# All steps of an attention and two-layer kernel in a new order, with the small key and query loads split by head

## The chip, the cores and the metric

The kernel runs on one core of one Trainium2 chip. TensorE (PE in the profile) multiplies matrices, VectorE (DVE), ScalarE (ACT) and GpSimd (POOL) work elementwise, and SyncE (SP) issues most of the DMAs. The metric is the time of one execution on the device in microseconds; the median of three runs before the change is 488.42 us (487.62 to 489.02).

## What is computed

All data is float32. First attention with rotary positions over 2 batches, 8 heads, 576 positions and 64 dimensions per head; then a gated product; then a second layer whose middle is a softmax gate and a normalization.

```python
q_rot, k_rot = (rotate(q), rotate(k))      # x1*cos - x2*sin, x1*sin + x2*cos
scores = np.matmul(q_rot, k_rot.transpose(0, 1, 3, 2)) / np.sqrt(D)
attn = np.exp(scores - np.max(scores, axis=-1, keepdims=True))
attn = attn / (np.sum(attn, axis=-1, keepdims=True) + 1e-09)
x = np.matmul(attn, v)                     # reshaped to [1152, 512]
x = (x @ w_a) * (x @ w_b) @ w_out          # 512 -> 1536 -> 512
h = x @ w_in                               # 512 -> 1024
e = np.exp(h - np.max(h, axis=-1, keepdims=True))
solu = h * e / (np.sum(e, axis=-1, keepdims=True) + 1e-09)
ln = (solu - mu) / np.sqrt(var + 1e-06) * g_ln
out = ln @ w_out2                          # 1024 -> 512
```

## The kernel before

**Tiles and stages.** Every matrix product is made of three: each operand is kept as a high part, rounded to TensorE's fast float32 form by a cast, and a low part, the difference between the operand and its high part, and high x high, high x low and low x high are summed. So each operand costs a cast (mostly on ScalarE) and a difference (on VectorE or GpSimd).

Attention goes through eight pairs of heads, u = 0 to 7, with nine blocks of queries each (72 blocks in all). A pair's 576 positions lie as four blocks of 128 for head A, one block "R" with the last 64 positions of both heads, and four blocks for head B. For a pair, SyncE loads keys, queries and values (`lk`, `lq`, `lv`); the rotation is three passes (`rk0` to `rk2` for keys, `rq0` to `rq2` for queries, lines 320, 325 and 327) on GpSimd or VectorE; the rotated queries are written twice side by side by a DMA (`qd`, line 334); keys are cast and differenced (`kh` line 345, `kl` line 356) and both are transposed by TensorE (`kA`, `qA`, `R`, `kB`, `qB`, lines 373 and 379). Per query block: the scores (`qk`, line 446), the row maximum on VectorE (`mx`, line 455), the exponential on ScalarE (`ex`, line 463), transposes (`tp`, line 476), the high part on ScalarE (`ph`, line 490), the low part on VectorE (`pl`, line 494), and then the product with the values (`pv`, line 525). A quotient and a split write the pair's result into the input x of the next layer (`xa`, `xb`, `xc`).

The first layer begins with three groups of weights multiplied plainly (`AB`, line 716, three column ranges each, 24 instructions a range). Each product has two halves in one of two PSUM buffers; ScalarE copies one half out (`ab`, line 820) and VectorE multiplies it with the other (`g`, line 823), which frees the buffer. The other nine groups use Strassen's scheme (`P1` to `P7`, line 943), for which sums and differences of the input are made once (`s1`, `s3`, `sb`, `s2a` and so on, line 747), cast (`sh`, line 860) and differenced (`sl`). Then comes the product with `w_out` (`X`, line 1013, in three column ranges of 12 steps). The second layer multiplies tile 0 of nine row tiles plainly (`H`, line 1038) and the other eight in pairs by Strassen's scheme (`Q1` to `Q7`, line 1131). Its weight differences are summed on VectorE (`u1` to `u4`, line 747, buffer `tfh`), cast (`uh`), negated (`un`, line 1067), and completed by a DMA that adds `tfh` to the negated high part (`ua`, line 1070, issued from GpSimd). There are four such adding DMAs; the two of one k share a `tfh`, and the next k's `tfh` takes the same memory. Each tile then goes through maximum, exponential, product, statistics and normalization (`hx`, `he`, `hm`, `hs`, `hn`, lines 1159 to 1185), transposes (`L`, line 1193), and the last product (`O`, line 1229).

**What sets the order.** Nothing is scheduled at run time or by the compiler. The string SCHEDULE names every step, `name.index` with a last `.1` where a step goes to GpSimd instead of VectorE, and the program is written in exactly that order; each engine takes its own instructions from it in turn, and SyncE its DMAs. Steps wait for each other by semaphores, so a step whose input is late holds up everything behind it on its engine. The string was put out by a planner that is not part of the kernel.

The start is written out before the schedule: the first loads go out from SyncE and ScalarE (lines 613 to 619), TensorE turns over an identity matrix as warm-up, and `rka` rotates blocks 0 to 4 of the first keys, `kha` casts them and `kla` makes their low part.

Of the kernel before, what the change touches and what calls it, by code (L numbers as in the profile page):

```python
# [20 lines left out]
B, H, S, D = 2, 8, 576, 64  # L21
# [6 lines left out]
REM = 512  # L28
# [7 lines left out]
wm1.0 cs.0 lv.0 wm2.0 rka0.0 ll.0 rka1.0 rka2.0 rqx0.0 kha.0 rqx1.0 rqx2.0 kla.0 kA_0.0 kA_1.0 rqa0.0 rqa1.0  # L36
rqa2.0 qdx.0 qda.0 qAx0.0 qA_0.0 R_0.0 qAh0.0 rkb0.0 rkb1.0 rkb2.0 khb.0 klb.0 rqb0.0 R_1.0 rqb1.0 wm3.0 qAl0.0
R_2.0 rqb2.0 qAh1.0 qk.0 qAl1.0 qdb.0 wm4.0 qk.1 mx.0 ex.0 rq0.1.1 mx.1 rk0.1 ex.1 qk.2 kB_0.0 kB_1.0 mx.2 ex.2
rq1.1 rq2.1.1 rk1.1 rk2.1.1 qk.3 mx.3 qB_0.0 qB_1.0 qB_2.0 tp.0 tp.1 qk.4 ph.0 ex.3 lv.1 ph.1 pl.0 mx.4 t4A_0.0
t4A_1.0 tp.2 qk.5 qd.1 ph.2 qA_0.1 kh.1 pl.1 tp.3 ex.4 qk.6 mx.5 qA_1.1 vh.0 t4A_2.0 kl.1.1 ex.5 pl.2 ld.0  # L40
qA_2.1 lk.2 rk0.2.1 mx.6 ph.3 pl.3 t4R_0.0 kB_0.1 kB_1.1 tp.4 ex.6 qk.7 mx.7 lq.2 t4R_1.0 t4R_2.0 tp.5 vl.0
kA_0.1 R_0.1 ph.4 pl.4 qk.8 ph.5 mx.8 kA_1.1 rk1.2.1 lk.3 pv00_0.0 ex.7 tp.6 rk2.2.1 pv00_1.0 R_1.1 qk.9 rq0.2.1
rq1.2.1 rq2.2.1 R_2.1 pl.5 pv01_0.0 qd.2 pv01_1.0 ph.6 pl.6 ex.8 mx.9 sa.0 pv00_2.0 qk.10 kh.2 rs_0.0 qB_0.1
lq.3 pv00_3.0 lv.2 ex.9 tp.7 kl.2.1 mx.10 pv01_2.0 pv01_3.0 qk.11 mx.11 rs_1.0 t4B_0.0 qB_1.1 qB_2.1 ex.10 qk.12
rs_2.0 ph.7 ex.11 pl.7 vh.1 tp.8 mx.12 t4B_1.0 t4B_2.0 ph.8 kA_0.2 rk0.3.1 ex.12 rq0.3.1 pl.8 vl.1.1 rq1.3.1
qk.13 tp.9 kA_1.2 ph.9 qA_0.2 mx.13 pl.9 rk1.3.1 rk2.3.1 qk.14 pv10_0.0 tp.10 tp.11 qA_1.2 lk.4 ex.13 ph.10
pv10_1.0 qA_2.2 pv11_0.0 mx.14 ph.11 pl.10 pv10_2.0 ex.14 pv11_1.0 pv11_2.0 pl.11 pv10_3.0 tp.12 t4R_0.1
# [36 lines left out]
pv00_1.6 mx.62 ex.61 vl.7.1 ex.62 p3.0 R_2.7 p4.0 tp.60 pv01_0.6 pv01_1.6 ph.60 qB_0.7 qk.63 sa.6 rs_0.6 qk.64
# [1237 lines left out]
```

## Time and profile before

| | |
|---|---|
| median of three runs | 488.42 us |
| profiled execution | 487.74 us |
| its span, first to last instruction | 485.8 us |
| TensorE busy | 469.9 us, 97% of the span |
| VectorE busy | 407.2 us, 84% |
| ScalarE busy | 349.7 us, 72% |
| GpSimd busy | 199.0 us, 41% |
| mean granted TensorE clock | 1.000 |
| moved by DMA | 48.04 MB, 99 GB/s on average |

The shares are averages over stages with different limits. Attention ends near 162 us, the plain products run from there to about 197 us, Strassen's products to 302, the product with `w_out` to 379, and the second layer to the end. TensorE's busy time counts an instruction until its modelled end, so a busy TensorE in attention is not TensorE at its peak: an instruction of 288 columns takes 183 ns on average there (58.7 us for 320 of them in the scores) and 147 ns in Strassen's products (31.6 us for 216).

### The profile page before, as it was taken

Reading aid. Unit: us, or ns where it says so; the run is one execution under the profiler, and the core shown is the slowest. Engines: PE = TensorE matmul, PEld = TensorE weight load, DVE = VectorE, ACT = ScalarE, POOL = GpSimd, SP = SyncE. Lnnn points to the kernel's source line nnn. Section 1 sums busy time; section 2 is a strip of 40 time slices with the busy share of each in tenths; the row PEclk is TensorE's granted clock in tenths of the full one; section 3 lists DMA queues with packets and bytes.
Section 4 is the critical chain, followed back from the end, with each engine's and each line's share of the span. In section 5 each row is a group of like instructions: output and inputs, shape, how many; then the busy total and the mean of one; then the engine's idle time right before and its main releaser. Section 6 shows DMA issues by size and latency. Waiting matters only on the chain.

```text
span 485.8 us, 8453 instructions
## 1 busy us (share of the span) xinstructions
PE 469.9 (97%) x3109; PEld 441.9 (91%) x3109; DVE 407.2 (84%) x617; ACT 349.7 (72%) x655; POOL 199.0 (41%) x171
## 2 busy tenths in 40 slices
PE   8899899999989989999999999999999989999996
PEld 7789899999989979999999999999999778888886
DVE  5999899999999769988786898776786999978671
ACT  4899899999989275767878888787896763535321
POOL 1798989779433240022225113222211475431100
PEclk9999999999999999999999999999999999999999
DMA  5624414222203403414235654245337520100011
GB/s 141 185 65 108 116 32 129 75 50 73 57 7 106 148 26 120 142 52 123 89 132 169 217 175 173 89 173 188 127 120 175 92 81 1 44 23 22 23 43 43
DMA packets 47506, 48.04 MB, mean 99 GB/s; under 512 B 23979, under 2 KB 40938, under 8 KB 46954
## 3 DMA queue, kind: packets, MB, share of 16 engines
q1 hardware_dynamic: 45946, 44.53, 29.5%
q0 software_dynamic: 576, 2.10, 2.4%
q10 hardware_dynamic: 944, 0.89, 0.6%
q8 instruction: 24, 0.39, 0.3%
q14 instruction: 16, 0.13, 0.1%
HBM read 39.01 MB, written 4.49 MB: 90 GB/s over the span
## 4 chain that ended last, share of the span: by engine, by line
PE 69%; DVE 9%; ACT 8%; POOL 6%; DMA 4%; issue 3%; ACTq 0%; SPq 0%; DVEq 0%; POOLq 0%
PE x L1013 11%; PE out L1229 10%; PE pb L943 9%; PE pc L943 6%; PE pa L943 6%; PE s L446 5%; PE pv L525 5%; PE h L1131 5%; PE ab L716 4%; PE t L476 3%; PE lt L1193 2%; PE hc L1131 2%; ACT e L463 2%; DMA hT<-tfh 2%; DVE pT L494 1%
## 5 line engine op out<-in xcount | busy, mean ns | idle before, releaser
L1013 PE MATMUL x<-gs,wx 128*128 128x384 f32 x432 | 75.2, 334 | 0.0
L1013 PEld LDWEIGHTS x<-gs,wx 128*128 128x128 f32 x432 | 74.9, 188 | 0.1
L446 PE MATMUL s<-kS,qS 128*128 128x288 f32 x320 | 58.7, 309 | 2.2 <-ACT e L463 2.1
L455 DVE TENSOR_REDUCE nm<-s 128x1 f32<-128x576 f32 x72 | 53.9, 750 | 2.0 <-PE s L446 0.9
L463 ACT ACTIVATE e<-s,nm 128x576 f32<-128x576 f32 x72 | 53.5, 744 | 2.5 <-DVE nm L455 2.2
L169 ACT ACTIVATE f<-f 128x1024 f32<-128x1024 f32 x48 | 50.9, 1062 | 0.9
L1229 PE MATMUL out<-wout,lnT 128*128 128x512 f32 (+1 forms) x240 | 51.5, 371 | 0.0
L446 PEld LDWEIGHTS s<-kS,qS 128*128 128x128 f32 x320 | 45.2, 189 | 4.3 <-ACT e L463 3.5
L494 DVE TENSOR_TENSOR pT<-t,pT 128x512 fp32r<-128x512 f32 x72 | 48.3, 682 | 0.8 <-ACT pT L490 0.2
L1229 PEld LDWEIGHTS out<-wout,lnT 128*128 128x128 f32 x240 | 41.4, 189 | 7.2
L525 PE MATMUL pv<-pT,V 128*128 128x288 f32 x288 | 46.5, 302 | 0.6 <-DVE pT L494 0.2
L490 ACT CAST pT<-t 128x512 fp32r<-128x512 f32 x72 | 40.7, 582 | 2.8 <-PE t L476 2.3
L476 PE MATMUL t<-ident,e 128*128 128x128 f32 x288 | 41.9, 274 | 0.2
L525 PEld LDWEIGHTS pv<-pT,V 128*128 128x128 f32 x288 | 39.9, 188 | 1.5 <-DVE pT L494 0.4
L716 PE MATMUL ab<-xT,wab 128*128 128x384 f32 x216 | 38.8, 336 | 1.7 <-DVE g L823 1.2
L716 PEld LDWEIGHTS ab<-xT,wab 128*128 128x128 f32 x216 | 37.3, 188 | 2.6 <-DVE g L823 1.8
L476 PEld LDWEIGHTS t<-ident,e 128*128 128x128 f32 x288 | 33.5, 141 | 2.5 <-DVE pT L494 1.1
L177 DVE SCALAR_TENSOR_TENSOR f<-raw,f 128x1024 int32<-128x1024 int32 x26 | 34.1, 1310 | 0.4
L179 DVE SCALAR_TENSOR_TENSOR f<-raw,f 128x1024 int32<-128x1024 int32 x26 | 32.5, 1248 | 0.4
L943 PE MATMUL pb<-sums_x,wT 128*128 128x288 f32 x216 | 31.8, 296 | 0.0
L943 PE MATMUL pa<-xT,wB 128*128 128x288 f32 x216 | 31.6, 295 | 0.0
L167 ACT ACTIVATE f<-raw 128x1024 f32<-128x1024 f32 x24 | 27.7, 1153 | 4.7 <-DMA raw<-in_moe_w_b_dram 2.2
(215 smaller groups left out, 1027.7 us busy)
## 6 DMA issues: line engine op xcount, KB each, us to landing
raw<-in_moe_w_out_dram SPq DMA_DIRECT2D x10, 1024.0 KB, 4.8
raw<-in_moe_w_a_dram SPq DMA_DIRECT2D x12, 512.0 KB, 3.6
raw<-in_moe_w_b_dram SPq DMA_DIRECT2D x24, 256.0 KB, 4.2
raw<-in_moe_w_in_dram SPq DMA_DIRECT2D x4, 1024.0 KB
kraw<-in_k_dram SPq DMA_DIRECT2D x16, 128.0 KB, 2.2
qd<-in_q_dram SPq DMA_DIRECT2D x16, 128.0 KB, 3.1
vraw<-in_v_dram SPq DMA_DIRECT2D x8, 256.0 KB
wd<-f SPq DMA_DIRECT2D x4, 512.0 KB
```

The costliest lines, as they stand in the source:

```text
L169: act.activation(_raw(t), _raw(t), AF.Copy, scale=2.0 ** -SHIFT)
L446: nc.tensor.matmul(s[:, c, :KC], qS[u % 2][:, a, off:off + P], kS[u % 2][:, h, c * KC:(c + 1) * KC], start=(m == 0), stop=(m == last),)
L455: nc.vector.tensor_reduce(t, ps[n][:, :, :KC], axis=AX.XY, op=ALU.max, negate=True)
L463: nc.scalar.activation(t.rearrange("p (c n) -> p c n", c=2), ps.pop(n)[:, :, :KC], AF.Exp, bias=nm.pop(n), accum_out=sums[u][:, i:i + 1],)
L476: nc.tensor.transpose(t[:, j, :], e[n][:, j * P:(j + 1) * P], ident)
L490: nc.scalar.copy(hi, src)
L494: nc.vector.tensor_tensor(lo, src, _raw(hi), op=ALU.subtract)
L525: nc.tensor.matmul(o[:, :KC], w[:, h, 4 if m == 8 else m % 4].rearrange("p a d -> p (a d)"), t[:, m, c * KC:(c + 1) * KC], start=(m == 0), ...
L716: nc.tensor.matmul(pab[f, t][:, m, :CW], wf[:, a, (kk, 4 + (kk + 2) % 4)[m], :], xT[kk][:, xa, t * CW:(t + 1) * CW], start=(kk == a == xa ...
L943: nc.tensor.matmul(dst[:, c, :KC], w[:, a, k * P:(k + 1) * P], x(k, xa)[:, c * KC:(c + 1) * KC], start=(fresh and k == a == xa == 0), stop ...
L1013: nc.tensor.matmul(px[t, m][:, :CW], w[:, a], r[:, ga], start=(f == 0 and a == ga), stop=(f == NF - 1 and a == 1),)
L1229: nc.tensor.matmul(po[i, part][:, cols], lnT[i][:, la, kk, :], w[:, a, cols], start=(kk == la == a == 0), stop=(kk == NK2 - 1 and la == 1),)
```

## The change

Three edits. The whole SCHEDULE string is replaced by another, which holds the same steps with three new ones (`rkr0` to `rkr2`) and some of them on the other of VectorE and GpSimd. The planner that put it out now takes the adding DMAs as a single file, one after the other; the planner is not in the kernel, so this shows in the string alone. The last rows of keys and queries of every pair are loaded by two DMAs of 64 rows, as those of pair 0 were before, instead of one of 128. And the rotation of the first keys' blocks 0 to 4 is taken apart into blocks 0 to 3 (`rka`) and block 4 (`rkr`).

```diff
@@ -287,9 +287,7 @@
-        if "R" in parts and u > 0:
-            eng.dma_start(out=t[:, 4, :], in_=src[b, h0:h0 + 2, REM:S, :])
-        elif "R" in parts:
+        if "R" in parts:
             for j in range(2):
                 eng.dma_start(out=t[64 * j:64 * j + 64, 4, :], in_=src[b, h0 + j, REM:S, :])
@@ -654,7 +652,8 @@
-        add(f"rka{j}.0", rope, nc.vector, 0, k0, "k", 0, 5, (j,))
+        add(f"rka{j}.0", rope, nc.vector, 0, k0, "k", 0, 4, (j,))
+        add(f"rkr{j}.0", rope, nc.vector, 0, k0, "k", 4, 5, (j,))
@@ -33,112 +33,112 @@
-wm1.0 cs.0 lv.0 wm2.0 rka0.0 ll.0 rka1.0 rka2.0 rqx0.0 kha.0 rqx1.0 rqx2.0 kla.0 kA_0.0 kA_1.0 rqa0.0 rqa1.0
...
+rka0.0 ll.0 rka1.0 cs.0 rka2.0 rkr0.0 rkr1.0 rkr2.0 rqx0.0 kha.0 rqx1.0 rqx2.0 wm1.0 wm2.0 rqa0.0 rqa1.0 kla.0
...
```

Of the steps that change their engine, these matter in attention: the first and last pass of pair 1's rotation (`rq0.1`, `rk2.1`) go from GpSimd to VectorE, the low part of pair 0's values (`vl.0`) from VectorE to GpSimd. Among the input's sums for Strassen's scheme four go from GpSimd to VectorE and one the other way.

At three places the order reads as follows. The first is ScalarE where the plain products begin, from the cast of the second group's weights (`wab`); `a` is the copy of a product's half, `sums_x` the cast of an input sum, `f` a step of unpacking weights. Before:

```order
L192 CAST wab_2650<-f 128x1024
L820 ACTIVATE a_0_2677<-ab_0_2504 128x384
L860 CAST sums_x<-sums_f_2642 128x576
L820 ACTIVATE a_1_2681<-ab_1_2652 128x384
L860 CAST sums_x<-sums_f_2640 128x576
L167 ACTIVATE f<-raw 128x1024
L169 ACTIVATE f<-f 128x1024
L820 ACTIVATE a_2_2748<-ab_2_2698 128x384
```

and in the changed kernel:

```order
L192 CAST wab_2667<-f 128x1024
L819 ACTIVATE a_0_2669<-ab_0_2494 128x384
L819 ACTIVATE a_1_2697<-ab_1_2671 128x384
L819 ACTIVATE a_2_2726<-ab_2_2700 128x384
L167 ACTIVATE f<-raw 128x1024
L169 ACTIVATE f<-f 128x1024 x2
L819 ACTIVATE a_0_2795<-ab_0_2735 128x384
L167 ACTIVATE f<-raw 128x1024
L859 CAST sums_x<-sums_f_2657 128x576
```

The two casts that stood between the three copies stand behind a fourth copy now.

The second is GpSimd from the cast of pair 1's values (`V`) to the rotation of pair 3; `t2k` and `t2q` are the first passes for keys and queries, `kraw` and `qd` the loaded keys and queries. Before:

```order
L347 CAST V_577<-vraw_326 128x10x64
L320 TENSOR_TENSOR t2k_3_594<-kraw_450,s_sb 128x576
L320 TENSOR_TENSOR t2q_3_598<-qd_518,s_sb 128x576
L365 TENSOR_TENSOR V_577<-vraw_326,V_577 128x10x64
L325 TENSOR_TENSOR qd_518<-qd_518,c_sb 128x9x64
L325 TENSOR_TENSOR kraw_450<-kraw_450,c_sb 128x576
```

and in the changed kernel:

```order
L345 CAST V_568<-vraw_440 128x10x64
L318 TENSOR_TENSOR t2k_3_577<-kraw_486,s_sb 128x576
L323 TENSOR_TENSOR kraw_486<-kraw_486,c_sb 128x576
L363 TENSOR_TENSOR V_568<-vraw_440,V_568 128x10x64
L318 TENSOR_TENSOR t2q_3_672<-qd_544,s_sb 128x576
L323 TENSOR_TENSOR qd_544<-qd_544,c_sb 128x9x64
```

The first pass over pair 3's queries has moved behind a pass over the keys and behind the values' low part.

The third is GpSimd around the four adding DMAs (`hT<-tfh`); `gs` is a low part for the product with `w_out`, the first number in its name the step it belongs to. Before:

```order
L747 TENSOR_TENSOR gs_5_4555<-g_2639,gs_5_4555 128x384
L747 TENSOR_TENSOR gs_6_4571<-g_3462,gs_6_4571 128x384
L1070 DMA hT_4577<-tfh_4529 128x1024
L1070 DMA hT_4537<-tfh_4529 128x1024
L1070 DMA hT_4732<-tfh_4714 128x1024
L1070 DMA hT_4739<-tfh_4714 128x1024
```

and in the changed kernel:

```order
L746 TENSOR_TENSOR gs_3_4537<-g_2654,gs_3_4537 128x384
L1069 DMA hT_4592<-tfh_4512 128x1024
L1069 DMA hT_4636<-tfh_4512 128x1024
L746 TENSOR_TENSOR gs_9_4666<-g_3744,gs_9_4666 128x384
L1069 DMA hT_4715<-tfh_4706 128x1024
L1069 DMA hT_4748<-tfh_4706 128x1024
```

The first two stand behind the low part of step 3 instead of step 6, and a low part of step 9 stands between the pairs. In the schedule the first comes four steps of the product before the second (`X.2.4` to `X.2.7`), where before it was two (`X.2.9` and `X.2.10`, with the first half of tile 0's product).

## Rows read from the trace of the kernel before

**Rows 1.** Windows: start:end, length, busy time (instructions) of each engine, clock, DMA
```profile
60.00:132.00 72.00, 71.22 (x574) 68.08 (x573) 69.60 (x121) 69.58 (x177) 57.06 (x45) 1.00 0.28 72
...
168.00:180.00 12.00, 10.32 (x57) 9.36 (x56) 7.12 (x10) 6.83 (x9) 6.47 (x4) 1.00 0.25 84
...
197.00:356.00 159.00, 159.00 (x1092) 158.51 (x1091) 130.62 (x159) 125.98 (x166) 40.38 (x30) 1.00 0.42 144
...
397.00:482.00 85.00, 84.91 (x427) 70.88 (x425) 64.03 (x108) 32.88 (x64) 22.06 (x29) 1.00 0.09 27
```
**Rows 2.** Chain of waits (first row) and timeline, the start: start, us, what
```profile
1.76 3.46 DMA kraw<-in_k_dram
...
5.35 0.49 DVE L320 TENSOR_TENSOR t2k<-kraw,s_sb 128x320 f32<-128x320 f32 x1 [3.78 <-DMA kraw<-in_k_dram]
...
6.16 0.40 ACT L341 COPY s_sb<-s_sb 128x256 f32<-128x256 f32 x1
...
6.93 0.46 ACT L345 CAST kd<-kraw 128x320 fp32r<-128x320 f32 x1 [0.37 <-DVE kraw L327]
```
**Rows 3.** Groups by line and form, VectorE, 0 to 180: busy us, mean ns, idle
```profile
L747 DVE TENSOR_TENSOR sums_f<-xT 128x1152 f32<-128x1152 f32 x2 | 2.7, 1354 | 0.1
...
L823 DVE TENSOR_TENSOR g<-ab,a 128x384 f32<-128x384 f32 x3 | 1.7, 552 | 4.7 <-ACT a L820 4.7
...
L195 DVE TENSOR_TENSOR wab<-f,wab 128x1024 fp32r<-128x1024 f32 x1 | 1.2, 1212 | 0.0
L365 DVE TENSOR_TENSOR V<-vraw,V 128x640 fp32r<-128x640 f32 x1 | 0.9, 930 | 0.0
...
L320 DVE TENSOR_TENSOR t2k<-kraw,s_sb 128x576 f32<-128x576 f32 x1 | 0.7, 749 | 0.0
...
L320 DVE TENSOR_TENSOR t2k<-kraw,s_sb 128x256 f32<-128x256 f32 x1 | 0.4, 425 | 0.0
...
L320 DVE TENSOR_TENSOR t2q<-qd,s_sb 128x64 f32<-128x64 f32 x1 | 0.2, 225 | 0.0
```
**Rows 4.** Timeline, GpSimd and TensorE, 38 to 53 us
```profile
38.59 1.44 POOL L320 TENSOR_TENSOR t2q<-qd,s_sb 128x576 f32<-128x576 f32 x1 [2.88 <-DMA qd<-in_q_dram]
...
52.64 0.54 PE L373 MATMUL qtkA<-ident_r,kd 128*128 128x128 f32 x4 [1.26 <-POOL kd L356]
```
**Rows 5.** Line 325 on GpSimd: ns min/median/max, first and last start
```profile
L325 POOL TENSOR_TENSOR kraw<-kraw,c_sb x6: 1409/1424/1432, 24.5 to 103.7; 128x576 f32<-128x576 f32 x6
```
**Rows 6.** Timeline, 166 to 180 us
```profile
166.66 3.75 POOL L747 TENSOR_TENSOR sums_f<-xT 128x1152 f32<-128x1152 f32 x1 [12.26 <-DMA raw<-in_moe_w_b_dram]
...
171.94 0.68 ACT L860 CAST sums_x<-sums_f 128x576 fp32r<-128x576 f32 x1 [4.66 <-POOL sums_f L747]
...
173.04 0.56 DVE L823 TENSOR_TENSOR g<-ab,a 128x384 f32<-128x384 f32 x1 [4.68 <-ACT a L820]
...
174.78 4.09 PE L716 MATMUL ab<-xT,wab 128*128 128x384 f32 x22 [0.51 <-DVE wab L195]
...
179.86 16.92 PE L716 MATMUL ab<-xT,wab 128*128 128x384 f32 x96 [0.99 <-DVE g L823]
```
**Rows 7.** Adding DMAs' landings (first row), then timeline, 376 to 394 and 470 us
```profile
DMA to landing us min/median/max: 4.6/4.9/7.6
...
376.13 1.29 DVE L747 TENSOR_TENSOR tfh<-f 128x512 f32<-128x512 f32 x2 [2.53 <-DMA hT<-tfh]
...
381.82 1.21 PE L1038 MATMUL h<-wh,x2T 128*128 128x512 f32 x4 [0.35 <-DVE wh L195]
...
390.68 2.92 DVE L1185 TENSOR_SCALAR et<-et,mv,rs 128x1024 f32<-128x1024 f32 x1 [0.21 <-POOL rs L1180]
...
393.65 1.09 PE L1193 MATMUL lt<-ident,et 128*128 128x128 f32 x8 [1.59 <-DVE et L1185]
...
470.38 0.81 DVE L1185 TENSOR_SCALAR et<-et,mv,rs 128x1024 f32<-128x1024 f32 x1 [0.73 <-POOL rs L1180]
```
**Rows 8.** Line 291's DMA issues on SyncE's queue: ns min/median/max, first and last
```profile
L291 SPq DMA_DIRECT2D kraw<-in_k_dram x7: 554/566/587, 10.5 to 93.0; - x7
```

More of the change, by code (lines that the diff above doesn't have):

```diff
@@ L141 @@
[L141 removed]
+rka0.0 ll.0 rka1.0 cs.0 rka2.0 rkr0.0 rkr1.0 rkr2.0 rqx0.0 kha.0 rqx1.0 rqx2.0 wm1.0 wm2.0 rqa0.0 rqa1.0 kla.0
+rqa2.0 qdx.0 kA_0.0 qAx0.0 qda.0 R_0.0 kA_1.0 rkb0.0 rkb1.0 rkb2.0 qA_0.0 rqb0.0 wm3.0 qAh0.0 qAl0.0 rqb1.0
+rqb2.0 lv.0 qdb.0 R_1.0 R_2.0 qk.0 wm4.0 qAh1.0 qAl1.0 mx.0 qk.1 ex.0 rq0.1 khb.0 klb.0 qk.2 kB_0.0 rk0.1 mx.1
+ex.1 qB_0.0 tp.0 mx.2 tp.1 ex.2 rk1.1 kB_1.0 rq1.1 lk.2 rk2.1 rq2.1.1 qk.3 ph.0 mx.3 pl.0 ph.1 pl.1 qk.4 kh.1
@@ new lines @@
+qk.11 vh.1 ph.7 t4B_0.0 t4B_1.0 rk0.3.1 rk1.3.1 tp.8 qk.12 mx.11 vl.1.1 pl.7 kA_0.2 tp.9 mx.12 ex.11 qk.13
+t4B_2.0 ph.8 pl.8 ph.9 pl.9 kA_1.2 qA_0.2 pv10_0.0 tp.10 mx.13 pv10_1.0 ex.12 qk.14 qA_1.2 qA_2.2 tp.11 pv11_0.0
+ph.10 pv11_1.0 pv10_2.0 rq0.3.1 rq1.3.1 rk2.3.1 pl.10 tp.12 mx.14 ld.0 ph.11 ex.13 pv11_2.0 pl.11 t4R_0.1 qk.15
+ph.12 pv10_3.0 kB_0.2 t4R_1.1 pv11_3.0 t4A_0.1 t4R_2.1 tp.13 mx.15 ex.14 xa.0.1 qk.16 kB_1.2 pl.12 t4A_1.1
+rq2.3.1 ex.15 qd.3 tp.14 pv00_0.1 ph.13 t4A_2.1 pv00_1.1 ph.14 qk.17 R_0.2 mx.16 ex.16 R_1.2 vh.2 kh.3 kl.3.1
@@ new lines @@
+pl.13 tp.15 ph.15 lk.4 pl.14 mx.17 ex.17 rk0.4.1 qk.18 mx.18 pv01_0.1 pv01_1.1 pv00_2.1 R_2.2 pv01_2.1 sa.1
+qB_0.2 pl.15 pv00_3.1 qk.19 pv01_3.1 lk.5 ex.18 rs_0.1 tp.16 lq.4 rs_1.1 qB_1.2 ph.16 tp.17 qk.20 xb.0 rk1.4.1
+rs_2.1 mx.19 ex.19 ph.17 rk2.4.1 qB_2.2 kA_0.3 t4B_0.1 vl.2.1 pl.16 kA_1.3 xc.0.1 mx.20 pl.17 t4B_1.1 qk.21
+tp.18 qA_0.3 ph.18 pv10_0.1 qA_1.3 t4B_2.1 mx.21 rq0.4.1 pv10_1.1 qA_2.3 ex.20 pv10_2.1 ex.21 tp.19 ph.19 qk.22
+qk.23 pl.18 tp.20 pv11_0.1 lv.3 pv10_3.1 kh.4 pv11_1.1 vh.3 mx.22 kl.4.1 lk.6 mx.23 pl.19 ex.22 ph.20 pl.20
@@ new lines @@
+rq0.7.1 pv11_0.4 ph.46 ph.47 ex.50 pv11_1.4 pv11_2.4 rk1.7.1 rk2.7.1 qk.51 pl.46 pl.47 mx.51 tp.48 t4R_0.5
+rq1.7.1 kh.7 rq2.7.1 ph.48 kB_0.6 pv11_3.4 qk.52 t4A_0.5 qd.7 t4R_1.5 t4R_2.5 tp.49 mx.52 pl.48 xa.4.1 xb.4
+xc.4.1 kB_1.6 tp.50 ex.51 t4A_1.5 qk.53 ex.52 R_0.6 R_1.6 t4A_2.5 pv00_0.5 ph.50 qk.54 mx.53 R_2.6 tp.51 ex.53
+ph.49 pl.50 ph.51 mx.54 pl.49 sa.5 pl.51 qk.55 pv00_1.5 mx.55 ex.54 rs_0.5 pv00_2.5 pv00_3.5 pv01_0.5 pv01_1.5
+pv01_2.5 pv01_3.5 ex.55 qk.56 qB_0.6 tp.52 rs_1.5 qB_1.6 ph.52 rs_2.5 kl.7.1 tp.53 ph.53 qk.57 mx.56 ex.56 vh.6
@@ new lines @@
+pa.19 gl.0.5.1 pb.19 pc.19 X.0.5 gl.1.2 gh.0.6 X.1.2 gh.1.3 gh.0.7 p2.19 gl.0.6 X.0.6 p3.19 gl.1.3 p4.19 hi.18
+X.1.3 hi.19 gh.1.4 gl.1.4.1 ld.20 lo.18 pa.20 gl.0.7 lo.19 gh.0.8 pb.20 pc.20 p2.20 X.0.7 gh.1.5 gl.1.5 p3.20
+gl.0.8.1 p4.20 X.1.4 ld.21 pa.21 gh.0.9 pb.21 pc.21 gl.0.9 X.0.8 gh.1.6 X.1.5 ld.22 X.0.9 p2.21 sc.20.1 gl.1.6
+sc.20.0 p3.21 gh.0.10 X.1.6 gh.1.7 p4.21 sc.21.1 so.20 sc.21.0 so.21 gl.0.10 gh.0.11 pa.22 gl.0.11.1 X.0.10
+gh.1.8 X.0.11 pb.22 xh.0.0 xl.0.0 xh.0.2 xl.0.2 pc.22 p2.22 gh.1.9 gl.1.9 p3.22 xh.0.1 xl.0.1 gl.1.7.1 X.1.7
@@ new lines @@
+X.2.8 gh.2.11 gl.2.11 gl.2.9.1 X.2.9 ri.10 S1a.1 u1.1 ri.12 u3.1 hi.24 lo.24 u2.1 uh.1.0 un.1.0 ua.1.0 S1b.1
+X.2.10 X.2.11 xl.1.3 u4.1 hi.25 uh.1.1 to_out H.0.0 Sh.1.1 H.0.1 un.1.1 ua.1.1 ri.20 xh.2.2 lo.25 S3a.1 S3b.1
+S2a.1.1 Sh.1.3 hj.10 H.0.2 H.0.3 Q1.1 xl.2.2 xh.2.0 hx.0 xl.2.0 xh.2.3 xl.2.3 Sl.1.3.1 S2b.1.1 Q7.1 S3a.3 he.0
+hm.0 Sh.1.2 Sl.1.2.1 S3b.3 q1.1 Q6.1 S4a.1.1 S4b.1.1 q7.1 Q4.1 S1a.3.1 hs.0 q6.1 Sh.1.4 hj.12 xh.2.1 Sl.1.4
+Sl.1.1 Q2.1 Q5.1 xl.2.1 hn.0 lj.10.1 ri.21 q5.1 L.0.0 L.0.1 hj.21 q4.1 lj.12.1 lh.0.0 ll.0.0 Q3.1 hx.1 Sh.3.3
@@ L142 @@
+hm.8 L.7.0 L.7.1 lh.7.0 O.6.1.0 ll.7.0 hs.8 lh.7.1 st.5.0 st.6.0 O.7.0.0 ll.7.1 hn.8 L.8.0 lh.8.0 ll.8.0 L.8.1
+lh.8.1 O.7.1.0 O.8.0.1 ll.8.1 O.8.1.1 st.7.0 O.8.0.2 O.8.1.2 st.8.1 st.8.2
 """
```

180 lines of the change are left out of this document (75 added, 105 removed).

## The prediction

> **What bounds the kernel now.** I read the table of windows first, then the waits inside the stretches that it singles out, then the timeline around each of those, and last the two orders. In the windows the reader should compare TensorE's busy time with the length of each stretch [rows 1]. From 197 to 356 us and from 397 to 482 us TensorE is busy 243.91 of 244 us at a granted clock of 1.00. It does the same matrix multiplications after the change, so no order of the other engines can gain time there; it can only lose some. In the attention part (60 to 132 us stands for it) TensorE is busy 71.2 of 72 us, but VectorE is busy 69.6 and ScalarE 69.6: three engines run nearly full, and what is there to gain is small gaps, VectorE's 2.4 us among them. Real holes are at four places: the start, which waits for loads [rows 2]; one late key operand near 52 us [rows 4]; the hand-over from attention to the first products, where TensorE is busy 10.3 of 12 us [rows 1, 6]; and the hand-over to the last layer near 376 to 394 us [rows 7]. The forecast is a sum over these four and a fifth term for what a new order can break.
>
> **The start and attention.** At the start VectorE's first key rotation covers five blocks and so waits for the last rows of the second head, which land at 1.76 + 3.46 = 5.22 us; it starts at 5.35, and ScalarE's cast of the rotated keys follows at 6.93, having waited 0.37 us for it [rows 2]. After the change three instructions over blocks 0 to 3 go first (0.425 us each, 1.28 us [rows 3]) and three over block 4 follow (0.225 us each, 0.68 us). Where the big load lands by 3.9 us, the last of the six ends near 5.9. ScalarE itself is busy until 6.56 with the doubled tables [rows 2], so the cast gains 0.37 us; where the big load lands no earlier than the small one, the three added instructions cost 1.96 us for six against 3 x 0.49 for three, or 0.48 us. The trace does not show its landing; the rows nearest are the two ends named, and I take a gain of 0.4, since the load was issued before the small ones.
>
> VectorE's load grows besides: two passes of the second pair's rotation come over from GpSimd (2 x 0.749), the low part of the first V goes there (0.930), and the split costs 0.48: together +1.05 us [rows 3]. All of it lies in the first 27 us, where some gaps take it; between 0 and 1.05 I take +0.5. In front of the second row maximum now stand two such passes instead of none, and the second of them needs the second pair's keys: the exponentials of the next query blocks are behind that wait, and TensorE's transposes behind them.
>
> GpSimd is the engine that made TensorE wait 1.26 us for the fourth pair's keys at 52.64 [rows 4]. It had itself waited 2.88 us at 38.59 for queries still on their way. In the new order the pass that waited has two others in front of it, the key product at 1.42 us [rows 5] and V's low part, a somewhat longer pass, and these fill the 2.88. Two passes fewer and one more stand ahead of the key operand as well. It comes some 4 us earlier, against a need of 1.26, so the wait goes: -1.26. What is late next is VectorE, which is full anyway. The part sums to -0.4 + 0.5 - 1.26 = -1.2 us. Its ends: -3.0 if the new order closes most of VectorE's 2.4 us as well, +2.5 if it opens as many new waits as there are now.
>
> **The hand-over to the products.** The cause of the hole can be read off as a chain [rows 6]. GpSimd makes a sum of 3.75 us at 166.66 and two more behind it. ScalarE stands 4.66 us before a cast of one of them, with the copy that frees the second product bank queued behind the cast. VectorE stands 4.68 us before that product, with the low half of the next weights queued behind it. TensorE then waits 0.51 us for the weights and 0.99 for a bank: 1.50 in all. In the new order ScalarE does all three copies before any cast, and GpSimd has one sum where it had three, so nothing stands behind its 3.75 us. VectorE has from 166.5 us: a sum of 1.35, the product of 0.55, two sums of 0.75, then the low half of the weights (1.21): done at 171.1, where TensorE now gets it at 174.78 after 0.51 us of waiting [rows 3, 6]. From then on each group of 24 takes TensorE 16.92 / 4 = 4.2 us. The second product (171.7) and the third (a 1.35, two 0.75 and 0.55 later, 175.1) free their banks ahead of the groups that need them, which begin near 173.7 and 177.9. VectorE takes on some 2.25 us of sums and has 4.68 to put them in. The third group of weights, by the same counting, comes within 0.1 us of its need, so I take 1.3 of the 1.50. The ends are -1.5 and +0.9, the latter if the wait does not take the 2.25 us of added sums and they come through to TensorE behind the 1.3 gained.
>
> **The hand-over to the last layer.** Two adding DMAs stand back to back on GpSimd; the slowest of the four takes 7.6 us from issue to landing where the median is 4.9. VectorE waits 2.53 us for it at 376.13 before it can refill the buffer, and TensorE 0.35 us for the weights' low half behind that [rows 7]. In the new order the first stands five steps of the x product earlier (behind `X.2.3`, not `X.2.8`) and four steps stand between the first two, at some 2 us each (12 instructions at the 0.17 us of the 128x384 products [rows 6]), so the two do not meet and VectorE's wait goes. But little of that reaches the end. TensorE's next wait, 1.59 us before the transposes at 393.65, ends with the normalization of tile 0 at 390.68 + 2.92. In the new order 128x512, 128x256 (three) and 128x384 (three) pieces stand on VectorE between the tile's maximum and that step, by the nearest rows 0.75 + 3 x 0.425 + 3 x 0.552 = 3.7 us; now it is one, two and one: 2.15 [rows 3]. So the chain starts about as much earlier as it has become longer. I take -0.2. The ends: -2.1 if the normalization takes 0.81 us as at 470.38 [rows 7] instead of 2.92, +1.5 if the start is not earlier.
>
> **What a new order can break.** In 244 us without a hole in TensorE every load, cast and difference is moved a little, and a few may come late. The nearest rows are the holes at the places above, 0.35 to 1.6 us each. Between 0 and 2 us I take +0.4.
>
> **The sum.** -1.2 - 1.3 - 0.2 + 0.4 = -2.3 us. The profiled execution took 487.74 us (span 485.8 and 1.9 around it), which gives 485.4; it lies 0.7 below the median of 488.42, and the forecast for the median is 488.42 - 2.3 = 486.1 us.
>
> **Rivals.**
> First, the last hand-over gains as well: the normalization runs beside no GpSimd work and takes its 0.81. For it: the rows of two lengths of one instruction. Against it: GpSimd's weight differences stand in the same place as before. It gives 486.1 - 2.1 = 484.0.
> Second, the start's new first passes hold up the first maxima, and attention, full on VectorE, pays the 1.05 us and gives the gain at 52 us back elsewhere: +1.0 in place of -1.2, 488.3, no change. For it: 96.7% on VectorE from 60 to 132 us. Against it: that hole in TensorE was made by GpSimd, and its load falls.
> Third, the slower one: the small loads. Fourteen more DMAs stand on the one queue from SyncE, 0.56 us each [rows 8], two for each pair of heads but the first, and each pair's queries land up to 1.12 us later. It decides where GpSimd comes to the rotation before the landing, as it did at 38.59 [rows 4]. With four of the seven pairs so, and each delay going through rotation, difference and transposes to TensorE, 4 x 1.12 = 4.5 us: 490.6. Against it: in the new order the rotations of queries stand several steps behind their loads. The Trainium skill ("DMA: Bandwidth & Descriptors", Bandwidth) speaks for it: "Transfers under 64 KB are descriptor-dominated", so that half the rows would save nearly nothing of a landing. The row at hand agrees as far as it goes: 16 KB took 3.46 us at the start [rows 2].
> Fourth, the change doesn't do what it says: the adding DMAs still meet. Then VectorE's 2.53 us stays, of which TensorE feels 0.35 and the chain behind it little more: 486.5.
>
> **Chances.** Forecast 0.48, first rival 0.13, second 0.20, third 0.15, fourth 0.04. What can be told from no change with this kernel is about 0.3%, 1.47 us: faster is below 486.95, slower above 489.89. Of the forecast's 0.48 (its own range 484.2 to 487.6) 0.38 lies below; of the second rival 0.03 below, 0.15 between and 0.02 above; of the third 0.14 above and 0.01 between; of the fourth half each below and between; the first all below. That is 0.56 faster, 0.28 no change, 0.16 slower. The range reaches from 483.0 to 489.8: it leaves out the third rival and the end of the first.
>
> **What would show it.** Right: the first VectorE rotation before 4.5 us and the cast of keys near 6.5; no wait of TensorE for GpSimd's key difference near 52; no wait of ScalarE for GpSimd's sums after 165 and TensorE busy through 168 to 180; four landings of about 4.9 us for the adding DMAs; the transposes of tile 0 still waiting for the normalization. Wrong: TensorE holes of over 2 us in all after 197 outside the last hand-over, GpSimd waiting for query loads at more than two pairs, or attention's end (the last group of the first product) no earlier than now. If the total is above 489.89, the third rival's waits have to be there, or the forecast has missed a mechanism.

## The result, and the profile of the changed kernel

The changed kernel takes 484.37 us (median of 6 runs, 482.95 to 484.85) against 488.10 for the kernel before on the same chip: ratio 0.991, interval 0.9884 to 0.9935, so 3.2 to 5.7 us faster. The forecast was 486.1 with a range of 483.0 to 489.8. The profiled execution took 484.39 us with a span of 482.4, 3.4 less than before. Faster was right; the gain is 1.6 times the forecast of 2.3 us, and it does not lie where the forecast put it.

The windows of the changed kernel, with the columns of [rows 1]:

```profile
60.00:132.00 72.00, 69.63 (x556) 66.36 (x555) 69.06 (x118) 67.08 (x170) 57.01 (x45) 1.00 0.29 73
168.00:180.00 12.00, 12.00 (x71) 11.95 (x71) 11.97 (x14) 6.23 (x9) 2.35 (x1) 1.00 0.24 82
197.00:356.00 159.00, 158.69 (x1090) 158.37 (x1090) 130.85 (x157) 127.28 (x168) 45.36 (x32) 1.00 0.42 146
397.00:482.00 85.00, 81.20 (x412) 68.15 (x410) 59.39 (x100) 30.03 (x58) 26.89 (x30) 1.00 0.10 28
```

The hole between 168 and 180 us is gone (10.32 before). From 60 to 132 us TensorE does less than before, 69.63 against 71.22: in attention something new is late. The last row ends early with the kernel.

The timeline of the start, then of GpSimd, SyncE's queue and TensorE in attention (start, duration, instruction, idle time before it and what ended it), against [rows 2, 4]:

```profile
3.60 0.42 DVE L318 TENSOR_TENSOR t2k<-kraw,s_sb 128x256 f32<-128x256 f32 x1 [2.02 <-DMA s_sb<-in_rope_cs_dram]
6.12 0.45 ACT L343 CAST kd<-kraw 128x320 fp32r<-128x320 f32 x1
12.07 0.74 ACT L461 ACTIVATE e<-s,nm 128x576 f32<-128x576 f32 x1 [1.30 <-DVE nm L453]
...
44.26 0.66 SPq L332 DMA_DIRECT2D qd<-qd  x1
44.96 1.40 SPq L287 DMA_DIRECT2D kraw<-in_k_dram  x2
46.41 1.12 SPq L292 DMA_DIRECT2D kraw<-in_k_dram  x2
50.75 1.43 POOL L318 TENSOR_TENSOR t2k<-kraw,s_sb 128x576 f32<-128x576 f32 x1 [3.84 <-DMA kraw<-in_k_dram]
...
89.22 1.42 POOL L318 TENSOR_TENSOR t2q<-qd,s_sb 128x576 f32<-128x576 f32 x1 [3.00 <-DMA qd<-in_q_dram]
...
101.80 0.72 POOL L345 CAST V<-vraw 128x640 fp32r<-128x640 f32 x1 [1.90 <-DMA vraw<-in_v_dram]
105.58 0.53 PE L371 MATMUL qtkA<-ident_r,kd 128*128 128x128 f32 x4 [0.85 <-POOL kd L354]
```

The cast of the first keys comes 0.81 us earlier, the first exponentials 1.57 us (13.64 before). TensorE's wait at 52.64 is gone. But GpSimd now waits 3.84 us for the fifth pair's keys, 3.00 for one pair's queries and 1.90 for the sixth pair's values, and behind the last of these TensorE waits 0.85 for a key difference.

TensorE at the hand-over to the products, against [rows 6], then the last hand-over, against [rows 7] (VectorE, the landings of the adding DMAs, TensorE):

```profile
159.59 2.66 PE L523 MATMUL pv<-pT,V 128*128 128x288 f32 x18
162.08 32.44 PE L715 MATMUL ab<-xT,wab 128*128 128x384 f32 x186
194.36 1.75 PE L942 MATMUL pa<-xT,wB 128*128 128x288 f32 x12
...
371.07 1.29 DVE L746 TENSOR_TENSOR tfh<-f 128x512 f32<-128x512 f32 x2
380.03 1.22 DVE L1158 TENSOR_REDUCE mx<-h 128x1 f32<-128x1024 f32 x1 [1.22 <-PE h L1037]
387.76 2.42 DVE L1184 TENSOR_SCALAR et<-et,mv,rs 128x1024 f32<-128x1024 f32 x1
...
387.25 5.18 POOL L746 TENSOR_TENSOR wout<-wout 128x1024 fp32r<-128x1024 f32 x2
...
DMA to landing us min/median/max: 4.5/4.6/4.9
...
390.24 1.09 PE L1192 MATMUL lt<-ident,et 128*128 128x128 f32 x8 [1.15 <-DVE et L1184]
```

The 186 plain multiplications run as one block. The first two adding DMAs are issued at 360.75 and 365.75 us and no longer meet. The last two, at 374.83 and 378.15, still overlap, since none lands in less than 4.5 us, but all four land in 4.5 to 4.9. VectorE refills the buffer without a wait. The transposes of tile 0 still wait for the normalization, 1.15 us instead of 1.59.

Three points on TensorE's timeline cut each execution into four stages: the end of the last `pv` block (before: 159.30 + 2.71), the first `pa` block (before: 196.62) and the first `lt` block. All lengths are in us, each from one profiled execution:

| kernel | attention | plain products | Strassen products to `lt` | last layer |
|---|---|---|---|---|
| before | 162.01 | 34.61 | 197.03 | 92.15 |
| changed | 162.25 | 32.11 | 195.88 | 92.16 |
| changed, second execution | 162.13 | 32.09 | 195.89 | 92.19 |

The differences are +0.2, -2.5, -1.15 and 0: together -3.4, the difference of the spans. In these two executions the last three stages repeat within 0.05 us; in the kernels below that share the order of the third stage it takes 195.85 to 196.32. Attention scatters more, as the experiments show. The profiled execution of the kernel before is a short one (487.74, median 488.10) and that of the changed kernel lies at its median, so the 3.4 is a little less than the 3.7 between the medians.

### The profile page after: what moved, and what is told of

It is laid out like the page before. It is cut to its first block, busy times and chain, and to the rows that moved or that the text cites. A ratio compares the mean times of both kernels' runs of the same rounds, so it can differ in the third digit from the quotient of the medians.

```text
span 482.4 us, 8477 instructions
## 1 busy us (share of the span) xinstructions
PE 468.2 (97%) x3109; PEld 442.3 (92%) x3109; DVE 411.4 (85%) x619; ACT 349.5 (72%) x655; POOL 203.7 (42%) x172
## 4 chain that ended last, share of the span: by engine, by line
PE 78%; DVE 8%; ACT 4%; DMA 3%; POOL 3%; SPq 2%; issue 2%; POOLq 0%; ACTq 0%
PE x L1012 15%; PE out L1228 10%; PE pb L942 9%; PE ab L715 8%; PE pc L942 6%; PE pa L942 6%; PE s L444 5%; PE pv L523 5%; PE t L474 4%; PE h L1130 3%; PE lt L1192 2%; SPq L287 1%; DVE nm L453 1%; PE hc L1130 1%; PE h L1037 1%
## 5 line engine op out<-in xcount | busy, mean ns | idle before, releaser
L177 DVE SCALAR_TENSOR_TENSOR f<-raw,f 128x1024 int32<-128x1024 int32 x26 | 33.0, 1268 | 0.4
L746 POOL TENSOR_TENSOR gs<-g,gs 128x384 fp32r<-128x384 f32 x13 | 16.0, 1237 | 39.5 <-ACT gs L991 39.4
L179 DVE SCALAR_TENSOR_TENSOR f<-raw,f 128x1024 int32<-128x1024 int32 x26 | 31.7, 1221 | 0.4
```

## Experiments

Each kernel was timed in five rounds beside the kernel before. Changes against the kernel before are differences of medians, with the ratio and its interval.

**Undoing one stage at a time.** In each of three kernels one stretch of the schedule is that of the kernel before, the rest that of the changed one. Steps that stand on the other side of a border in the two orders are done once, behind the border. The first kernel also has the loads and the first rotation as before.

```diff
 e1: the order up to to_ffn
 e2: the order from to_ffn to to_x
 e3: the order from to_x to the end
-<that stretch of the changed kernel's SCHEDULE>
+<that stretch of the SCHEDULE before>
```

> Attention and start of the kernel before, everything from the hand-over to the products on as in the changed kernel. Theory A (ledger read from the two traces: attention 0, hand-over to the products -2.2, last hand-over with what the order breaks -1.0): as fast as the changed kernel, 3.0 to 3.7 us below the kernel before. Rival B (the terms as the prediction had them, -1.2, -1.3, +0.2): 1.0 to 1.5 us below the kernel before, that is 2 us slower than the changed one. Rival C (the stretches only work together, since the hand-over finds other engines late): no faster than before.

> Attention and the last layer of the changed kernel, and between them the old order from the first weight sums up to the start of the x product. Theory A: the hole of 2.2 us between attention and products is back and the last hand-over keeps its gain, so 1.0 to 1.4 us below the kernel before. Rival B: 1.3 of the gain is lost, and it stays 2 us or more below before. Rival C: no faster than before.

> Attention, hand-over and products of the changed kernel, and from the x product on the old order with two adding DMAs back to back. Theory A: 2.2 to 2.5 us below the kernel before; VectorE again waits about 2.5 us for the adding DMA and the first transposes come about 1.1 us later than in the changed kernel, relative to the end of the products. Rival B: the last hand-over is worth 0.2 us, so 3.2 us or more below before. Rival C: no faster than before.

Measured: -3.5 us with the old attention (0.9935, 0.9917 to 0.9952), -2.7 with the old hand-over (0.9951, 0.9934 to 0.9967), -3.2 with the old last part (0.994, 0.9924 to 0.9955). Each is worth less than the whole, and no stretch needs another to work, so rival C falls. The totals alone don't separate A from B: the first (2.4 to 4.1 us by its interval) speaks for A and against B, the second (1.6 to 3.2) misses A's 1.0 to 1.4, and the third (2.2 to 3.7) allows both. The stages do. With the old hand-over the plain products take 34.31 us again, with the old last part the third stage takes 197.95. That one's VectorE and TensorE:

```profile
374.48 1.29 DVE L744 TENSOR_TENSOR tfh<-f 128x512 f32<-128x512 f32 x2 [3.00 <-DMA hT<-tfh]
380.17 1.21 PE L1035 MATMUL h<-wh,x2T 128*128 128x512 f32 x4 [0.80 <-DVE wh L193]
392.03 1.10 PE L1190 MATMUL lt<-ident,et 128*128 128x128 f32 x8 [1.57 <-DVE et L1182]
```

Attention ends at 161.19 and 161.99 in the two kernels that have the changed one's, a spread of 0.8 us for one order; in the one with the old attention the granted clock was 0.86 from 156 to 168 us, so its end (164.40) isn't compared. Its worth in the totals is the 0.3 to 0.9 us by which the first kernel falls short, less than the intervals.

**The loads of attention.** The first kernel loads the last rows of both heads by one DMA again, the second moves two groups of loads ahead of the copies behind which they stood, the third does both. The fourth is the changed kernel again.

```diff
 e4, e10
-        if "R" in parts:
+        if "R" in parts and u > 0:
+            eng.dma_start(out=t[:, 4, :], in_=src[b, h0:h0 + 2, REM:S, :])
+        elif "R" in parts:
 e6, e10: SCHEDULE
-rq1.3.1 rk2.3.1 pl.10 tp.12 mx.14 ld.0 ph.11 ... qd.3 ... lk.4 ...
+rq1.3.1 rk2.3.1 pl.10 tp.12 mx.14 ld.0 lk.4 ph.11 ... qd.3 ...
-kl.5.1 lk.7 ex.38 ... qd.6 ... lv.5 vh.5 ...
+kl.5.1 lk.7 lv.5 ex.38 ... qd.6 ... vh.5 ...
```

> The changed kernel with the last rows of both heads loaded by one DMA again for all pairs but the first (14 DMAs fewer). Theory A: the halved loads are hidden, within 0.5 us of the changed kernel (3.0 to 4.0 below before). Rival D (the prediction's third rival in small: each pair's queue is 1.1 us longer, and part of the lead that attention loses between 100 and 116 us is lost to loads issued late): 1 to 2 us below the changed kernel, with GpSimd's 1.9 us wait for the sixth V gone.

> The changed kernel, unaltered, beside the next three on one chip. It should come 3.5 to 4.5 us below the kernel before. Theory A2 (the lead of the start is partly given back in attention to loads of keys and values that land late, and how late varies from execution to execution): the exponentials of a second profiled execution differ from the first by up to 1 us after the fourth pair's keys, with GpSimd again waiting 3.4 to 4.2 us for keys near 50 us. Rival (the attention part is worth nothing, as read from the first pair of profiles): its end lies at the same place as before, within 0.2 us.

> The changed kernel with two groups of loads issued ahead of the copy of rotated queries that they stood behind on SyncE: the fifth pair's keys (behind the first product weights) and the sixth pair's V. Theory A2: GpSimd's waits of 3.84 us at 50.75 and 1.90 us at 101.80 go, TensorE's 0.85 us wait for the key difference at 105.58 goes too, and attention ends 0.8 to 1.5 us earlier; the total is 0.8 to 1.5 us below the changed kernel. Rival E (VectorE, full at 69 of 72 us, sets the pace of attention, and GpSimd's waits are idle time off the path): within 0.3 us of the changed kernel.

> The changed kernel with both the two early groups of loads and one DMA for the last rows of both heads. Theory A2 (both edits take away the same late landings): 1.3 to 2.0 us below the changed kernel, at most 0.5 better than either alone, attention's last exponentials 2.3 to 2.8 us earlier. Rival J (two separate causes that add up): 2.5 us or more below the changed kernel.

Measured: -5.6 us with one load (0.9881, 0.9864 to 0.9899), -4.0 for the changed kernel again (0.9917, 0.9899 to 0.9935), -5.7 with early loads (0.9889, 0.9865 to 0.9912), -7.0 with both (0.9844, 0.9824 to 0.9864). Of the single edits each interval just meets or overlaps that of the changed kernel, so the traces have to tell. GpSimd with early loads, and the window that holds most of attention:

```profile
46.98 1.42 POOL L316 TENSOR_TENSOR t2k<-kraw,s_sb 128x576 f32<-128x576 f32 x1
...
59.27 0.72 POOL L343 CAST V<-vraw 128x640 fp32r<-128x640 f32 x1 [3.08 <-DMA vraw<-in_v_dram]
...
98.70 1.19 POOL L343 CAST V<-vraw 128x640 fp32r<-128x640 f32 x1
...
60.00:132.00 72.00, 70.34 (x561) 67.03 (x561) 69.94 (x120) 67.71 (x173) 56.71 (x44) 1.00 0.29 73
```

Both waits are gone, and so is TensorE's at the key difference; attention ends at 160.00, 2.2 us earlier. The exponentials show where that comes from: up to the 22nd they start within 0.15 us of those of the changed kernel, from the 23rd some 0.8 us earlier, from the 29th 1.2, and from the 50th 2.2. GpSimd waits 3.08 us at 59.27 instead, for values, so not every wait of GpSimd's for a load comes through. This execution is also the shortest of its six; by the medians of the spans (481.0 against 482.4) the edit is worth 1.4 us. Rival E falls. In the changed kernel the chain of work that ended last runs through the late keys (start, duration, what):

```profile
42.83 1.40 POOL qd L325
...
46.94 3.69 DMA kraw<-in_k_dram
...
50.75 1.43 POOL t2k L318
...
55.70 0.67 ACT kd L343
```

GpSimd ends a rotation at 44.2, SyncE can then issue the copy of those queries, and only then the keys behind it in the queue, which GpSimd waits for next. The Trainium skill ("DMA: Bandwidth & Descriptors", Anatomy of one DMA) says that a semaphore wait for a DMA happens on the issuing sequencer before dispatch; the copy at 44.26 with the keys' loads at 44.96 right behind it agrees. With one load for both heads the keys' queue is shorter by 0.55 us and the wait ends 0.86 us earlier:

```profile
49.89 1.43 POOL L320 TENSOR_TENSOR t2k<-kraw,s_sb 128x576 f32<-128x576 f32 x1 [3.42 <-DMA kraw<-in_k_dram]
...
99.76 0.72 POOL L347 CAST V<-vraw 128x640 fp32r<-128x640 f32 x1 [1.39 <-DMA vraw<-in_v_dram]
```

There attention ends at 160.20, in the shortest of four executions (spans 480.4 to 481.9). The total speaks for rival D, but the wait for the sixth pair's values, which D had gone, is still 1.39.

In the second execution of the changed kernel TensorE's granted clock was 0.96 of full speed on average from 12 to 60 us (0.50, the lower of its two levels, from 16 to 18). Its exponentials from the fourth to the 22nd started 1.3 us later than in the first execution, from the 23rd 0.9, and from the 29th to the 40th 0.1 to 0.2; from the 41st they were 0.8 to 0.9 late once more, and from the 50th 0.1 early. Its chain, too, runs through the fifth pair's keys (48.12, 3.44 us to the landing). So a delay ahead of these places did not come through to the end.

```profile
12.00:60.00 48.00, 45.19 (x345) 42.50 (x344) 44.10 (x75) 43.50 (x110) 38.88 (x31) 0.96 0.45 115
...
51.67 1.42 POOL L318 TENSOR_TENSOR t2k<-kraw,s_sb 128x576 f32<-128x576 f32 x1 [3.48 <-DMA kraw<-in_k_dram]
```

Its rival, that attention is worth nothing, holds for this execution too (162.13), but not for the order: the two kernels above, with the same attention, ended at 161.19 and 161.99. The two edits together gain 3.0 us over the changed kernel, each taken against the kernel before on its own chip. That is near the sum of 1.6 and 1.7, so the totals speak for rival J. The profile can't confirm it: it caught the longest of that kernel's five runs (483.86 where the others are 481.84 to 482.22), with TensorE waiting 1.1 us for a copy of queries. This version beats both kernels.

**The split loads alone, in the order before.**

```diff
-        if "R" in parts and u > 0:
-            eng.dma_start(out=t[:, 4, :], in_=src[b, h0:h0 + 2, REM:S, :])
-        elif "R" in parts:
+        if "R" in parts:
```

> The kernel before with nothing changed but the last rows of queries and keys loaded head by head (14 DMAs more). The prediction's third rival: each pair's queries land up to 1.1 us later, and with every one of these delays passed on it is 3 to 4.5 us above the kernel before. Theory A2 (a late landing costs only where GpSimd already waits for it, once or twice): 0.3 to 1.5 us above. Theory K (hidden): the same within 0.3 us.

Measured: -0.5 us (0.9982, 0.997 to 0.9994, 12 runs): not slower. GpSimd's wait for queries in [rows 4] grows by 0.33 us, and TensorE's wait behind it by 0.17; a third pair's queries are waited for as well:

```profile
39.46 1.43 POOL L318 TENSOR_TENSOR t2q<-qd,s_sb 128x576 f32<-128x576 f32 x1 [3.21 <-DMA qd<-in_q_dram]
...
53.53 0.54 PE L371 MATMUL qtkA<-ident_r,kd 128*128 128x128 f32 x4 [1.43 <-POOL kd L354]
...
73.30 1.43 POOL L318 TENSOR_TENSOR t2q<-qd,s_sb 128x576 f32<-128x576 f32 x1 [1.58 <-DMA qd<-in_q_dram]
```

Both theories with a price fall, and the 14 DMAs are hidden or slightly better in that order. They seem to cost something only in the new one, where loads stand close behind a copy; why they should gain here is open.

**The hand-over to the products: copies without sums.** In the kernel before, the casts move behind the third copy, VectorE's two differences behind them move after the third product, and the sums stay where they were.

```diff
-ab.0.0 g.0.0 sh.2.0 ab.0.1 g.0.1 ... sh.0.0 lo.1 ... sl.2.0 s2a.1 sl.0.0 AB.0.2 AB.1.0 ab.0.2 g.0.2
+ab.0.0 g.0.0 ab.0.1 g.0.1 ... lo.1 ... s2a.1 AB.0.2 AB.1.0 ab.0.2 sh.2.0 sh.0.0 g.0.2 sl.2.0 sl.0.0
```

> The kernel before with one piece of the new order alone: at the hand-over to the products ScalarE makes all three copies before the two casts that wait for GpSimd's sums, and VectorE's two differences behind those casts come after the third product. Theory L (the casts in front of the copies make the hole): TensorE's wait of 0.99 us for a bank goes, and of the 1.50 us in both waits 0.8 or more goes; total 0.6 to 1.8 us below the kernel before. Rival M (the sums on GpSimd make it, wherever the casts stand): both waits remain or move to the next group, and the total is the same within 0.3 us.

Measured: -1.3 us (0.998, 0.9962 to 0.9997, 12 runs). TensorE at this place:

```profile
162.82 15.77 PE L714 MATMUL ab<-xT,wab 128*128 128x384 f32 x90
179.10 4.46 PE L714 MATMUL ab<-xT,wab 128*128 128x384 f32 x24 [0.51 <-DVE g L821]
183.75 4.45 PE L714 MATMUL ab<-xT,wab 128*128 128x384 f32 x24 [0.19 <-DVE g L821]
188.45 8.56 PE L714 MATMUL ab<-xT,wab 128*128 128x384 f32 x48 [0.25 <-DVE g L821]
```

The first 90 multiplications run without a hole, but the bank comes late afterwards, three times: the plain products take 33.86 us, 0.75 less than before of the 2.5 that the whole order gains. There VectorE waits for one of GpSimd's sums ahead of the third product:

```profile
171.48 4.85 POOL L745 TENSOR_TENSOR sums_f<-sums_f 128x576 f32<-128x576 f32 x2
176.36 0.76 DVE L745 TENSOR_TENSOR sums_f<-sums_f,xT 128x576 f32<-128x576 f32 x1 [1.33 <-POOL sums_f L745]
```

So the casts make the first hole (theory L), and by this wait the sums on GpSimd keep a later one open (rival M); copies alone bring about a third of the stage's gain. Of the 1.50 us in the two waits of [rows 6] less went than L had asked for: 0.95 is waited again. The profiled execution is one of the long ones of this kernel (489.60, the shortest 486.96), and its third stage takes 1.5 us more than before, with new holes of 0.27 and 0.34 us near 286 and 292. So it doesn't show where the -1.3 of the total comes from.

**The adding DMAs.** Two kernels put the first beside the second.

```diff
 e8
-un.0.1 ... ua.0.1 gl.2.6 ... un.0.0 ... xl.1.1 ua.0.0
+un.0.1 ... gl.2.6 ... un.0.0 ... xl.1.1 ua.0.1 ua.0.0
 e9
-un.0.1 ... ua.0.1 gl.2.6 ... un.0.0 ... xl.1.1 ua.0.0
+... gl.2.6 ... un.0.1 un.0.0 ... xl.1.1 ua.0.1 ua.0.0
```

> The changed kernel with the first adding DMA moved down to stand directly ahead of the second on GpSimd, near 365 us, so that two are under way together. Theory H (the single file is what brings the last hand-over its gain): the slower landing is 7 us or more, VectorE waits 2 to 3 us for it before refilling the buffer, and the first transposes come 0.5 us or more later than in the changed kernel; total 0.3 to 1.0 us above it. Rival I (the gain there comes from the order of VectorE's pieces and the fewer casts ahead of the maximum): VectorE waits, but the transposes still wait for the normalization at the same place, and the total is within 0.3 us of the changed kernel.

> The changed kernel with the first adding DMA's seed on ScalarE moved down beside the second's, so that the two adding DMAs are issued within 1.5 us of each other near 366 us. Theory H (the single file is what the last hand-over gains by): the slower of the two lands 7 us or more after its issue, VectorE waits 2.0 to 3.5 us for it at 371, TensorE waits 0.5 us or more for the weights' low half behind it, and the total is 0.7 to 1.5 us above the changed kernel (3.0 to 3.8 below the kernel before becomes 2.5 to 3.3). Rival I (order of VectorE's pieces alone): VectorE waits 2 us or more but TensorE's waits stay at 0.39 and 1.15 us, and the total is within 0.3 us of the changed kernel.

The first edit did nothing to GpSimd: no other instruction of its stands between the two, so the DMA is issued as soon as its seed is there, at 361.5, and the landings are 4.5 to 5.2 us. It is the changed kernel a third time, -3.9 us (0.9913, 0.9893 to 0.9933), and tells nothing of H or I. The second holds back the seed, and the two DMAs are issued at 364.35 and 365.53. Measured: -2.5 us (0.9934, 0.9917 to 0.9951), so 1.2 to 1.5 us slower than the changed kernel (-3.7 to -4.0 in its three measurements).

```profile
DMA to landing us min/median/max: 4.5/4.8/8.1
...
373.73 1.29 DVE L744 TENSOR_TENSOR tfh<-f 128x512 f32<-128x512 f32 x2 [3.04 <-DMA hT<-tfh]
376.21 3.02 PE L1035 MATMUL h<-wh,x2T 128*128 128x512 f32 x12 [0.31 <-DVE wh L193]
379.45 1.19 PE L1035 MATMUL h<-wh,x2T 128*128 128x512 f32 x4 [0.23 <-DVE wh L193]
383.18 1.20 PE L1128 MATMUL hc<-hT,sx 128*128 128x512 f32 x4 [0.48 <-POOL sx L744]
392.32 1.10 PE L1190 MATMUL lt<-ident,et 128*128 128x128 f32 x8 [1.66 <-DVE et L1182]
```

VectorE waits 3.04 us, and TensorE at five places for 3.2 us in all (0.54 at 384.92 not shown) where the changed kernel has 1.54. The third stage takes 198.43 instead of 195.9. Theory H holds, by the totals at the upper end of its price and by the stage at more; rival I falls.

**The normalization.**

```diff
-... S2b.1.1 ... S1a.3.1 hs.0 ... hn.0 lj.10.1 ri.21 ... lj.12.1
+... S2b.1.1 lj.10.1 ... hs.0 ... hn.0 lj.12 S1a.3 ri.21 ...
```

> The changed kernel with GpSimd kept idle beside the normalization of the last layer's first tile: one difference of output weights earlier on GpSimd, the other and one sum of 128x512 behind the normalization on VectorE. Theory F (the prediction's first rival: the normalization is long because GpSimd works beside it): it takes 0.8 to 1.2 us instead of 2.42, TensorE's 1.15 us wait before the first transposes falls below 0.4, and the total is 0.7 to 1.2 us below the changed kernel. Rival G (its length has another cause, or the added 1.9 us on VectorE comes through): the wait stays above 0.8 us and the total is the same within 0.5 us or higher.

Measured: -3.2 us (0.9931, 0.9913 to 0.9949), 0.8 us slower than the changed kernel on the same chip, with overlapping intervals.

```profile
381.49 2.39 POOL L744 TENSOR_TENSOR wout<-wout 128x1024 fp32r<-128x1024 f32 x1
...
382.34 2.08 DVE L744 TENSOR_TENSOR sf<-x2T 128x512 f32<-128x512 f32 x1
...
385.06 1.19 PE L1128 MATMUL h<-hT,sx 128*128 128x512 f32 x4 [0.75 <-POOL sx L744]
...
389.47 0.81 DVE L1182 TENSOR_SCALAR et<-et,mv,rs 128x1024 f32<-128x1024 f32 x1
390.19 1.22 DVE L744 TENSOR_TENSOR wout<-wout 128x1024 fp32r<-128x1024 f32 x1
391.33 0.68 DVE L744 TENSOR_TENSOR sf<-x2T 128x512 f32<-128x512 f32 x1
...
392.76 1.62 PE L1128 MATMUL h<-wh,sx 128*128 128x512 f32 x6 [1.33 <-DVE hs L1148]
```

The normalization takes 0.81 us and TensorE doesn't wait for it, but the first transposes come no earlier (third stage 195.95 against 195.88). The sum of 128x512 that now meets GpSimd's difference takes 2.08 us where it took 0.68, and TensorE waits 0.75 us for a sum that stands behind that difference on GpSimd. A step later TensorE waits 1.33 us for VectorE, where the difference and the sum that were moved behind the normalization (1.22 and 0.68) stand ahead of the operand. F's mechanism holds and G has the total: the cost was moved. The Trainium skill ("SBUF — State Buffer", Who interferes with whom) states that VectorE and GpSimd share a pair of ports: a VectorE instruction in a 2-port mode contends for it, and one side blocks for a whole instruction of the other; one with two inputs in SBUF contends with a GpSimd instruction that reads SBUF. The rows agree: the 2.08 ends 0.54 us behind the end of GpSimd's 2.39, and the changed kernel's 2.42 lies beside the first of two differences (5.18 for both).

## Why the prediction came out as it did

- **The start.** First rotation at 3.60 and cast at 6.12: right, and 0.81 us where 0.4 was taken. Of it 0.37 is the wait that the prediction named; another 0.35 comes from ScalarE itself, which began its first work at 3.91 instead of 4.26, and that was not in the term.
- **Attention, -1.2.** The wait at 52.64 went, as predicted. The step that failed is "What is late next is VectorE, which is full anyway". Next was GpSimd again, at the keys and values queued behind a copy of rotated queries. The profiled end came no earlier (162.25 against 162.01), which the prediction had named as a sign against itself; over the seven profiled executions with this order it is 161.2 to 162.5. The old order scatters too: in the kernel with the copies moved, whose attention is that of the kernel before, it ended at 162.98. So by these ends and the totals above attention gained something between nothing and some 0.9 us, not 1.2; no run pins it down. That is near the second rival's outcome, with another cause. Early loads get 2.2 us back in the profile and 1.4 by the medians of the spans. The +0.5 for VectorE's added work is not shown by itself in any run.
- **The hand-over to the products, -1.3.** The mechanism was right, the size was -2.5, beyond the end of -1.5. The term was the sum of two waits, 1.50. The stage held another 1.0: a wait of 0.17, and 0.82 by which TensorE's busy time for the same 186 multiplications fell, from 11.63 + 0.62 + 4.09 + 16.92 = 33.26 to 32.44. That is 0.27 for each of the three restarts, in the blocks and not in a wait. The kernel with the copies moved agrees: 24 multiplications behind a restart take 4.45 us there, where 24 of the single block take 32.44 x 24 / 186 = 4.19.
- **The last hand-over, -0.2.** The step that failed is "the chain starts about as much earlier as it has become longer". From the maximum to the end of the normalization it grew by 0.5 us (380.03 to 390.18, before 383.99 to 393.60), not by 1.5: the normalization starts 1.0 us later behind the maximum, and is itself 0.5 shorter (2.42, before 2.92). Measured from the first `pa` block, the maximum came 1.7 us earlier. The single file brings it: with the first two adding DMAs meeting, the stage loses 2.5 us. The first rival (0.81 us) did not come about: 2.42.
- **What a new order can break, +0.4.** 0.3 us from 197 to 356, nothing in the last layer.
- **The slower rival, small loads.** Refuted in the old order. In the new one they cost some 1.3 to 1.6 us by the medians, with intervals that just meet. Which load costs it is open: with one load for both heads GpSimd's waits for keys, values and one pair's queries are 0.42, 0.51 and 1.00 us shorter.

That the total lies in the range is in part luck: by the stages attention missed by +1.4 us, the products by -1.2 and the last hand-over with what the order breaks by -1.35, and these partly cancel.

## What to carry to other kernels

Size a hole by the length of its stage at full density, not by the sum of the waits shown in it. When a late operand goes away, look at what its engine waits for next and which in-order queue that load stands in: here a copy that waits for a rotation held up loads that needed nothing. Transfers that add in place are better kept apart than bunched where a buffer's refill waits for the slower one.

## What the runs showed of the hardware that was not expected

Two adding DMAs of 128x1024 issued some 1.2 us apart took up to 8.1 us to land; those issued 3.3 us or more apart took 4.5 to 5.2. A VectorE instruction beside a GpSimd one grew threefold (0.68 to 2.08, 0.81 to 2.42), and clearing one of them moved it to another. The time outside the span was 1.8 to 2.1 us in the other profiled executions and 3.0 in that with early loads (483.12 against 480.1).
